# Attention into a mish FFN on one core: another order for the opening, one weight piece in halves, a third probability buffer

## The chip, the cores and the metric

One core of one Trainium2 chip runs the whole program. The metric is the device time of one execution in microseconds (us). Five engines work side by side, each through its own list of instructions in order: TensorE (PE in the profile, with PEld for its weight loads), VectorE (DVE), ScalarE (ACT), GpSimd (POOL) and SyncE (SP), which issues the transfers.

## What is computed

Windowed attention over 8 sequences of 576 tokens with 8 heads of 64, then an FFN of 512 to 2048 to 512 with the activation h * tanh(softplus(h)), called mish in the kernel:

```python
    scores = scale * np.matmul(q, k.transpose(0, 1, 3, 2))
    mask = (rel >= 0) & (rel < window)          # rel = query - key, window = 64
    attn = exp(scores - max);  attn = attn / (sum + 1e-09)
    x = (attn @ v), as [4608 tokens, 512]
    h = x @ w_in                                 # w_in [512, 2048]
    g = h * np.tanh(softplus(h))
    out = g @ w_out                              # w_out [2048, 512]
```

The weights reach the kernel as 64-bit floats, and it decodes them itself.

## The kernel before

The 4608 tokens are cut into 12 chunks of 384 tokens. Per chunk there are four attention units, one for each pair of heads; unit i belongs to chunk i // 4 and pair i % 4. A unit runs in these steps (names of the cost table in brackets): scores on PE (`scores`), masking with the row's extreme on DVE (`ttr`, six of 128 columns), exp with the row sum on ACT (`exp`), a reciprocal of the sums (`small`) and the normalisation of the probabilities on DVE (`norm3` for three blocks of 128, `norm6` for six), the transpose of the probabilities (units 0 to 11 on PE, `tr`, and a copy out of PSUM, `pT`; later units by DVE and 12 small transfers), values on PE (`values`), and the split of x into a high part on ACT (`xh`) and a low part on DVE (`xl`), since every large product is made of three products of rounded parts.

The FFN goes over 16 weight pieces f. Piece f holds 128 columns of w_in and the matching 128 rows of w_out. For each chunk c and piece f: h(c,f) is 12 matmuls into one of two PSUM banks (line L440; `hcc` is one quarter of it, the three matmuls that need one pair's x), mish on ACT, the split of the result (g, `gh` and `gl`), and 9 matmuls that add to the chunk's sum (L514, `acc`). Chunk 0 sums into the banks acc, chunk 1 into the banks at, which the attention of the opening uses as well.

A piece is decoded once, in the opening, and stays: `abs` on ACT (L248) or `absv` on DVE (L251), a clamp (L253), a shift (L254), two merges with the words as they came (L256 and L261), a copy of the high part on ACT (L268) and the low part on DVE (L271). wa0 and wa1 are the two work buffers of the decoding. Exp and abs share one table of ACT and mish has another, so that ACT loads a table between them.

From chunk 2 on PE's order is written out by hand. For chunks 0 and 1 it is made by a planner (`Plan.order`): it steps through all operations with the costs in `COST`, gives each free engine the ready operation of the lowest rank, and the order in which operations would start becomes the order of each engine's list. Ranks come from `RANK_U` (attention units), `RANK_W` (pieces) and `r_ffn` (h and sums). `BEHIND[f]` says how many h of chunk 1 stand in the sequence once h(0,f) is in it; `ACT_ABS` is the number of pieces whose absolute value ACT takes; `SWITCH` is the rank that a table load costs an operation. The probabilities lie in a ring of two buffers (`pr0`, `pr1`), and the output rows in three (`o0` to `o2`).

Of the kernel before, what the change touches and what calls it, by code (L numbers as in the profile page):

```python
# [138 lines left out]
def tile_window_attn_mish_ffn(  # L139
# [24 lines left out]

    class Ring:
        def __init__(self, name, n, shape, dtype=F32, space=None):
            self.name = name
            self.tiles = [(space or const).tile(shape, dtype, name=f"{name}{i}", tag=f"{name}{i}") for i in range(n)]
            self.bufs = [Buf() for _ in range(n)]
# [59 lines left out]
    def weights(f, rank, on_act):  # L229
        buf = wbufs[f]  # L230
        a, abuf = wa_ring.take()
        af = a.bitcast(F32)
# [12 lines left out]
        load = add("SP", "issue", load, writes=[buf], rank=rank - 1.5, size=P * 2 * WP * 8,  # L245
                   after=pace or [units[f].scored])
        if on_act:
            x = add("ACT", "abs", lambda: nc.scalar.activation(af, words[1].bitcast(F32), AF.Abs),  # L248
                    reads=[buf], writes=[abuf], rank=rank, table="exp")
        else:  # L250
            x = add("DVE", "absv", lambda: nc.vector.tensor_scalar(a, words[1], 0x7FFFFFFF, None, ALU.bitwise_and),  # L251
                    reads=[buf], writes=[abuf], rank=rank)
# [510 lines left out]
```

## Time and profile before

| what | us |
|---|---|
| median of three runs | 922.49 |
| lowest and highest run | 921.87, 923.55 |
| the profiled execution | 922.28 |
| its span, first to last instruction | 920.5 |
| PE busy in the span | 900.1 (98%) |
| DVE, ACT, POOL busy | 315.7, 357.2, 262.1 |
| table loads on ACT after the first | 57, 73.1 us |

The profiled execution lies 0.21 us below the median and 1.78 us above its own span. Start times in the rows below count from the first instruction. A row of the timeline has start, duration, engine, line, operation, output and inputs, the number of instructions, and in brackets the idle time of the engine before it and what ended it. Durations of PE's rows overlap, since matmuls are pipelined; the differences of start times are what counts. A row of busy time by stretch has its length, busy time of PE, PEld, DVE, ACT and POOL with the number of instructions, the granted PE clock, the share of the transfer engines and GB/s.

### The profile page before, as it was taken

How to read it: one execution, taken by the hardware profiler on the slowest of the kernel's cores; microseconds unless marked ns; L12 is line 12 of the kernel's file. 1: busy time of each engine (PE TensorE's matmuls, PEld its weight loads, DVE VectorE, ACT ScalarE, POOL GpSimd, SP SyncE). 2: the span in 40 equal slices, each digit the busy share in tenths (PEclk: the TensorE clock that was granted, in tenths of full speed). 3: DMA queues.
4: the chain of work that ended last, by engine and by line, in shares of the span. 5: the costliest groups of instructions: out<-in, count | busy, mean ns of one | idle time of the engine just before them, and what ended most of it. 6: DMA issues, size and time to landing. Idle time of an engine off the chain costs nothing.

```text
span 920.5 us, 17007 instructions
## 1 busy us (share of the span) xinstructions
PE 900.1 (98%) x6411; PEld 808.2 (88%) x6411; DVE 315.7 (34%) x970; ACT 357.2 (39%) x958; POOL 262.1 (28%) x337
## 2 busy tenths in 40 slices
PE   6889999999999999999999999999999999999998
PEld 4678998888898998899899989998998999899897
DVE  6989973432314404304124034042141240400000
ACT  6885336744634414415225134143242241411110
POOL 1000000023333323433353244233333532432432
PEclk9799999999999999999999999999999999999999
DMA  8654412222324203312312222132122220110000
GB/s 272 222 200 168 158 72 73 90 81 71 103 59 127 84 20 95 111 26 88 115 28 83 67 82 78 56 94 77 61 88 67 77 82 24 52 37 1 35 1 35
DMA packets 79906, 77.28 MB, mean 84 GB/s; under 512 B 10064, under 2 KB 73296, under 8 KB 77776
## 3 DMA queue, kind: packets, MB, share of 16 engines
q1 hardware_dynamic: 79680, 75.96, 26.0%
q8 instruction: 51, 0.84, 0.4%
q14 instruction: 31, 0.25, 0.1%
q10 hardware_dynamic: 144, 0.23, 0.1%
HBM read 56.10 MB, written 9.44 MB: 71 GB/s over the span
## 4 chain that ended last, share of the span: by engine, by line
PE 92%; DVE 4%; DMA 2%; ACT 2%; issue 0%; SPq 0%; ACTq 0%; DVEq 0%
PE h L440 43%; PE acc L514 39%; PE at L514 4%; PE at L323 2%; PE at L414 2%; DMA st<-w 2%; PE h L414 1%; ACT pr L348 1%; DVE pr L344 1%; PE acc L323 1%; DVE wa L256 1%; DVE pr L357 0%; DVE wa L261 0%; ACT L723 0%; PE h L323 0%; PE acc L414 0%
## 5 line engine op out<-in xcount | busy, mean ns | idle before, releaser
L440 PE MATMUL h<-xh,w 128*128 128x384 f32 x1536 | 407.4, 338 | 2.0 <-ACT t L469 1.5
L514 PE MATMUL acc<-w,g 128*128 128x512 f32 x1224 | 287.8, 390 | 0.0
L440 PEld LDWEIGHTS h<-xh,w 128*128 128x128 f32 x1536 | 280.7, 189 | 7.1 <-ACT t L469 3.2
L514 PEld LDWEIGHTS acc<-w,g 128*128 128x128 f32 x1224 | 229.2, 188 | 48.0 <-issue 0.5
L469 ACT ACTIVATE t<-h 128x384 f32<-128x384 f32 x192 | 94.3, 492 | 448.4 <-PE h L440 448.1
L440 PE MATMUL h<-xl,w 128*128 128x384 f32 x768 | 258.6, 337 | 0.0
L481 POOL TENSOR_SCALAR gx<-t 128x384 fp32r<-128x384 f32 x40 | 20.5, 514 | 563.6 <-ACT t L469 213.9
L440 PEld LDWEIGHTS h<-xl,w 128*128 128x128 f32 x768 | 145.5, 189 | 2.2
L483 POOL TENSOR_TENSOR g<-t,g 128x384 fp32r<-128x384 f32 x120 | 130.5, 1088 | 9.8
L344 DVE CUSTOM_DVE_ANT_0 pr<-at,mask 128x128 f32<-128x128 f32 x150 | 34.6, 285 | 245.4 <-PE at L323 245.4
L514 PE MATMUL acc<-w,gx 128*128 128x512 f32 x360 | 91.4, 398 | 0.0
L481 POOL TENSOR_SCALAR g<-t 128x384 fp32r<-128x384 f32 x120 | 66.8, 557 | 70.2 <-PE acc L514 41.7
L348 ACT ACTIVATE pr<-pr,mx 128x128 f32<-128x128 f32 x204 | 79.3, 391 | 7.4 <-DVE mx L344 7.2
L514 PEld LDWEIGHTS acc<-w,gx 128*128 128x128 f32 x360 | 65.9, 188 | 15.2 <-issue 2.9
L723 ACT ACT_TABLE_LOAD x57 | 73.1, 1283 | 1.0
L344 DVE CUSTOM_DVE_ANT_0 wa<-at,mask 128x128 f32<-128x128 f32 x57 | 13.3, 286 | 126.1 <-PE at L323 126.1
L519 DVE COPY o<-acc 128x512 f32<-128x512 f32 (+1 forms) x22 | 14.4, 654 | 97.0 <-PE acc L514 94.6
L483 POOL TENSOR_TENSOR gx<-t,gx 128x384 fp32r<-128x384 f32 x40 | 40.5, 1013 | 3.3
L357 DVE TENSOR_TENSOR pr<-pr,sm 128x768 f32<-128x768 f32 (+1 forms) x38 | 40.6, 1068 | 0.9
L348 ACT ACTIVATION_READ_ACCUMULATOR pr<-pr,mx 128x1 f32 x204 | 38.4, 188 | 0.0
L323 PE MATMUL at<-k_t,q_t 64*64 64x128 f32 x828 | 34.8, 284 | 2.5 <-DMA k_t<-kT 1.3
L514 PE MATMUL at<-w,g 128*128 128x512 f32 (+1 forms) x147 | 35.7, 392 | 0.0
(71 smaller groups left out, 579.3 us busy)
## 6 DMA issues: line engine op xcount, KB each, us to landing
v_t<-vN SPq DMA_DIRECT2D x48, 384.0 KB, 4.0
st<-w SPq DMA_DIRECT2D x16, 1024.0 KB, 4.9
k_t<-kT SPq DMA_DIRECT2D x47, 224.0 KB, 4.2
q_t<-qT SPq DMA_DIRECT2D x48, 192.0 KB, 4.3
out<-o SPq DMA_DIRECT2D x35, 256.0 KB, 2.3
pT<-pr SPq DMA_DIRECT2D x288, 24.0 KB, 1.8
pT<-wa SPq DMA_DIRECT2D x144, 24.0 KB, 1.8
k_t<-kT ACTq DMA_DIRECT2D x1, 224.0 KB, 3.4
```

The costliest lines, as they stand in the source:

```text
L323: nc.tensor.matmul(t[par * BLK:(par + 1) * BLK, col:col + P], u.q[0][rows, n * BLK:(n + 1) * BLK], u.k[0][rows, n * BLK:n * BLK + P], star ...
L344: x = add("DVE", "ttr", lambda: nc.vector.tensor_tensor_reduce(out=pr[:, j, :], in0=t_s[:, col:col + P], in1=mk, op0=ALU.add, op1=ALU.min, ...
L348: return add("ACT", "exp", lambda: nc.scalar.activation(pr[:, j, :], pr[:, j, :], AF.Exp, bias=mx[:, j:j + 1], scale=-1.0, accum_out=sm[:, ...
L357: return add("DVE", "norm3" if n == NM else "norm6", lambda: nc.vector.tensor_tensor(pr[:, js, :], pr[:, js, :], sm[:, js].unsqueeze(2).to ...
L414: mm = nc.tensor.matmul(o_ps[rows, n * BLK:(n + 1) * BLK], v_t[:, n, rows], pT[:, 2 * par:2 * par + 2, h * NM + m, :], start=True, stop=True)
L440: nc.tensor.matmul(h_ps[:, :CH], ws[f][:, 0, part, cc * P:(cc + 1) * P], xx[:, cc, :], start=cc == 0 and i == 0, stop=cc == NPAIR - 1 and ...
L469: add("ACT", "mish", lambda: nc.scalar.activation(t, h_ps[:, :CH], AF.Mish), reads=[hb], writes=[tb], rank=post, table="mish")
L481: x = add("POOL", "poolgh", lambda: nc.gpsimd.tensor_scalar(g[:, 0, :], t, 1.0, 0.0, ALU.mult, ALU.add), reads=[tb], writes=[gb], rank=post)
L483: add("POOL", "poolgl", lambda: nc.gpsimd.tensor_tensor(g[:, 1, :], t, g[:, 0, :].bitcast(F32), ALU.subtract), reads=[tb], writes=[gb], af ...
L514: nc.tensor.matmul(bank[:, lo:hi], g[:, a, t * P:(t + 1) * P], ws[f][:, 1, n, lo:hi], start=(alone or f == 0) and i == 0, stop=(alone or f ...
L519: return add(eng, 0.15 + (hi - lo) / 1024, lambda: copy(o[:, lo:hi], bank[0][:, lo:hi]), reads=[bank[1]], writes=[ob], rank=-1)
L723: nc.scalar.preload_act_table_set(TABLES[t.load])
```

## The change

All of it lies in what feeds the planner and in chunks 0 and 1.

- New ranks for units and pieces, `BEHIND` with five h of chunk 1 right after h(0,2), costs of 1.05 instead of 1.2 for PE in the first 70 us, `SWITCH` 150 instead of 80.
- Piece 1 is loaded and decoded in two halves of 512 columns, first the w_in half, then the w_out half (`SPLIT`, `RANK_V`). h waits for the first half of a piece, the sum for the second.
- More h blocks are issued by quarters, each with its own wait for one pair's x (`HCC`).
- The pieces whose absolute value ACT takes are a list: 1, 3, 7, 10, 12 to 15. DVE has the others, pieces 0 and 2 among them.
- Units 2 and 3 are normalised on ACT in six instructions of 128 columns (`NORM_ACT`). Which engine copies a transposed tile is set unit by unit (`COPIES`).
- The three output buffers become one tile, and its first 768 columns serve as a third probability buffer until chunk 0 is done (`spare`).
- Fillers: matmuls of the identity, 64 columns wide, into an unused corner of an h bank, where the planner sees PE idle between 10 and 75 us of its own time; ten in all.

The cut diff:

```diff
-SLOW_UNTIL, SLOW = 70.0, 1.2
+WARM = 10.0, 75.0
+SLOW_UNTIL, SLOW = 70.0, 1.05
...
-SWITCH = 80.0
+SWITCH = 150.0
...
-    o_ring = Ring("o", 3, [P, DO])
-    wa_ring = Ring("wa", 2, [P, 2 * WP], U32)
+    o_ring = Ring("o", 1, [P, 3 * DO])
+    spare = o_ring.tiles[0][:, :HM * P]
+    o_ring.tiles, o_ring.bufs = [o_ring.tiles[0][:, i * DO:(i + 1) * DO] for i in range(3)], [Buf() for _ in range(3)]
+    pr_ring.extend([spare], [Buf()])
+    wa_ring = Ring("wa", 2, [P, 2 * WP], U32, parts=2)
...
+        halves = [[0], [1]] if f in SPLIT else [[0, 1]]
+        for half, rank in zip(halves, ranks):
+            part(f, half, rank, on_act, a, af, abufs, tiles, pace)
...
+            if u.n in NORM_ACT:
+                for j in range(js.start, js.stop):
+                    x = add("ACT", "normb", lambda j=j: nc.scalar.activation(
+                        pr[:, j, :], pr[:, j, :], AF.Copy, scale=sm[:, j:j + 1]), after=[x], rank=rank, reads=[mxb, smb])
+                return x
...
-                x = add("PE", "hcc", lambda cc=cc: emit(cc), reads=[xbufs[c % 2][cc], wbufs[f]], writes=[hb],
+                x = add("PE", "hcc", lambda cc=cc: emit(cc), reads=[xbufs[c % 2][cc], wbufs[f][0]], writes=[hb],
...
-                          reads=[gb, wbufs[f]], writes=[acc[t][1] for t in part], rank=rank, chain=chain,
+                          reads=[gb, wbufs[f][1]], writes=[acc[t][1] for t in part], rank=rank, chain=chain,
...
+    SPLIT = (1,)
+    ACT_ABS = (1, 3, 7, 10, 12, 13, 14, 15)
+    HCC = ((0, 0), (0, 1), (0, 2), (0, 3), (1, 0), (1, 2), (1, 3))
-    RANK_U = [0, 1, 4, 6, 2, 3, 16, 36]
+    RANK_U = [31.4, 31.7, 24.9, 51.0, 12.2, 55.7, 42.6, 55.1, 141.9, 163.3, 136.7, 197.1]
...
+    COPIES = [x.split() for x in ("DVE DVE", "DVE ACT", "ACT ACT", "ACT ACT", "DVE DVE", "ACT ACT", "ACT ACT", "DVE ACT", "ACT DVE", "ACT ACT", "DVE DVE", "ACT DVE")]
+    NORM_ACT = (2, 3)
...
-    ACT_ABS = 7
...
-    BEHIND = [max(0, min(f, 6), f - 8) for f in range(NF)]
+    BEHIND = [0, 1, 5, 5, 5, 5, 7, 7, 7, 8, 8, 8, 8, 8, 8, 8]
...
-        ffn_in(c, f, r_ffn(c, f), False, c == 0 and f < 2)
+        ffn_in(c, f, r_ffn(c, f), False, (c, f) in HCC)
...
+        if t.engine == "PE" and WARM[0] < t.start < WARM[1]:
+            for _ in range(int(0.6 * t.idle / COST["warm"])):
+                nc.tensor.matmul(H[0][0][:, CH:CH + BLK], ident, ident[:, :BLK], start=True, stop=True)
```

The new program has its own line numbers: L369 for the masking, L276 to L297 for the decoding, L387 for the normalisation on DVE, L408 for transposes, L413 for their copies, L444 for values, L458 for xl, L470 for h, L499 for mish, L507 and L508 for g, L544 for the sums, L754 for table loads.

Three places in the lists show the moves. The first is DVE around the normalisation of unit 7, the last of chunk 1 (`pr` is its probability buffer, `st` a piece as it came, `w` the finished piece). Before:

```order
L261 SCALAR_TENSOR_TENSOR wa_115<-st,wa_115 128x1024
L253 TENSOR_SCALAR wa_116<-wa_116 128x1024
L254 TENSOR_SCALAR wa_116<-wa_116 128x1024
L256 SCALAR_TENSOR_TENSOR wa_116<-st,wa_116 128x1024
L354 TENSOR_SCALAR sm_101<-sm_101 128x6
L355 RECIPROCAL sm_101<-sm_101 128x6
L261 SCALAR_TENSOR_TENSOR wa_116<-st,wa_116 128x1024
L357 TENSOR_TENSOR pr_96<-pr_96,sm_101 128x768
```

Now, at the same place in DVE's list:

```order
L281 SCALAR_TENSOR_TENSOR wa_113<-st,wa_113 128x1024
L458 TENSOR_TENSOR xl_118<-at_124,xh_117 128x384
L285 SCALAR_TENSOR_TENSOR wa_113<-st,wa_113 128x1024
L279 TENSOR_SCALAR wa_114<-wa_114 128x512
L379 TENSOR_SCALAR sm_101<-sm_101 128x6
L380 RECIPROCAL sm_101<-sm_101 128x6
L281 SCALAR_TENSOR_TENSOR wa_114<-st,wa_114 128x512
L387 TENSOR_TENSOR pr_95<-pr_95,sm_101 128x768
```

The end of piece 2 and the whole of piece 3 stood ahead of the normalisation (L357); now it is the end of piece 2 and a part of piece 1's second half (L387).

The second place is PE from the transposes of unit 7 to its values. Before (h of piece 2 for chunk 0 stands between, then values, then the sum of piece 1):

```order
L378 MATMUL at_126<-ident,pr_96 128x128 x3
L378 MATMUL at_124<-ident,pr_96 128x128 x3
L440 MATMUL h_127<-xh_117,w 128x384
L440 MATMUL h_127<-xl_118,w 128x384
L440 MATMUL h_127<-xh_117,w 128x384 x2
L440 MATMUL h_127<-xl_118,w 128x384
L440 MATMUL h_127<-xh_117,w 128x384 x2
L440 MATMUL h_127<-xl_118,w 128x384
L440 MATMUL h_127<-xh_117,w 128x384 x2
L440 MATMUL h_127<-xl_118,w 128x384
L440 MATMUL h_127<-xh_117,w 128x384
L414 MATMUL at_125<-pT_104,v_t_94 64x64 x12
```

Now:

```order
L408 MATMUL at_124<-ident,pr_95 128x128 x3
L408 MATMUL at_122<-ident,pr_95 128x128 x3
L470 MATMUL h_125<-xh_115,w 128x384
L470 MATMUL h_125<-xl_116,w 128x384
L470 MATMUL h_125<-xh_115,w 128x384 x2
L470 MATMUL h_125<-xl_116,w 128x384
L470 MATMUL h_125<-xh_115,w 128x384
L470 MATMUL h_126<-xh_117,w 128x384
L470 MATMUL h_126<-xl_118,w 128x384
L470 MATMUL h_126<-xh_117,w 128x384
L444 MATMUL at_123<-pT_104,v_t_94 64x64 x12
```

Instead of a whole h of chunk 0, half of one (h_125) and a quarter of h(1,0) stand there (h_126, with chunk 1's xh_117 and xl_118).

The third place is ACT behind the opening, where mish and the copies of the split follow each other (t is mish's output). Before:

```order
L469 ACTIVATE t_106<-h_127 128x384
L268 CAST w<-wa_115 128x2x512
L477 CAST g_109<-t_106 128x384
L469 ACTIVATE t_107<-h_128 128x384
L477 CAST g_110<-t_107 128x384
L469 ACTIVATE t_108<-h_127 128x384
L268 CAST w<-wa_116 128x2x512
```

Now:

```order
L499 ACTIVATE t_106<-h_125 128x384
L507 CAST g_109<-t_106 128x384
L754 ACT_TABLE_LOAD
L273 ACTIVATE wa_114<-st 128x1024
L294 CAST w<-wa_113 128x2x512
L754 ACT_TABLE_LOAD
L499 ACTIVATE t_107<-h_126 128x384
L507 CAST g_110<-t_107 128x384
```

An absolute value (L273) with a table load on each side now stands between two mish; there are six such places among the later pieces, and 66 table loads in the program where there were 58, the first one counted.

More of the change, by code (lines that the diff above doesn't have):

```diff
@@ L163, in tile_window_attn_mish_ffn, with joined, __init__ @@
     ctx.enter_context(tc.manual_schedule())
+    def joined(bufs):
+        b = Buf()
+        b.writers, b.readers = [t for x in bufs for t in x.writers], [t for x in bufs for t in x.readers]
+        return b
     class Ring:
[L166 to L169, printed above, removed]
+        def __init__(self, name, n, shape, dtype=F32, parts=1):
+            self.tiles = [const.tile(shape, dtype, name=f"{name}{i}", tag=f"{name}{i}") for i in range(n)]
+            self.bufs = [[Buf() for _ in range(parts)] if parts > 1 else Buf() for _ in range(n)]
             self.next = 0
@@ L243, in load, with cost @@
                 tc.add_manual_dep(d.ins, t.ins.name, SYNC, reason="pace")
-        load = add("SP", "issue", load, writes=[buf], rank=rank - 1.5, size=P * 2 * WP * 8,
-                   after=pace or [units[f].scored])
+        def cost(name):
+            return COST[name] if n == 2 else 0.05 + COST[name] / 2
+        add("SP", "issue", load, writes=bufs, rank=rank - 1.5, size=P * n * WP * 8, after=pace or [units[f].scored])
         if on_act:
-            x = add("ACT", "abs", lambda: nc.scalar.activation(af, words[1].bitcast(F32), AF.Abs),
-                    reads=[buf], writes=[abuf], rank=rank, table="exp")
-        else:
-            x = add("DVE", "absv", lambda: nc.vector.tensor_scalar(a, words[1], 0x7FFFFFFF, None, ALU.bitwise_and),
-                    reads=[buf], writes=[abuf], rank=rank)
@@ L253, in weights @@
-        x = add("DVE", "ts", lambda: nc.vector.tensor_scalar(af, af, BIG, TINY, ALU.min, ALU.max), after=[x], rank=rank)
-        x = add("DVE", "ts", lambda: nc.vector.tensor_scalar(a, a, 3, 0x3FFFFFFF, ALU.logical_shift_left, ALU.bitwise_and),
+            x = add("ACT", cost("abs"), lambda: nc.scalar.activation(af, words[1].bitcast(F32), AF.Abs),
+                    reads=bufs, writes=abufs, rank=rank, table="exp")
+        else:
+            x = add("DVE", cost("absv"), lambda: nc.vector.tensor_scalar(a, words[1], 0x7FFFFFFF, None, ALU.bitwise_and),
+                    reads=bufs, writes=abufs, rank=rank)
@@ L257, in weights @@
                 after=[x], rank=rank)
[L258 removed]
         def low():
[L261 to L264 removed]
+            task.ins = nc.vector.scalar_tensor_tensor(a, words[0], 29, a, ALU.logical_shift_right, ALU.bitwise_or).ins
+        x = task = used[f] = add("DVE", cost("stt"), low, after=[x], rank=rank)
         def high():
[L267 to L268 removed]
@@ L270, in weights @@
-        x = add("ACT", "wh", high, after=[x], rank=rank, reads=[abuf])
-        add("DVE", "stt", lambda: nc.vector.tensor_tensor(ws[f][:, :, 1, :], af2, ws[f][:, :, 0, :].bitcast(F32), ALU.subtract),
-            after=[x], rank=rank, reads=[abuf], writes=[buf])
-        return load
+            t = const.tile([P, n, 2, WP], F32R, name="w", tag=tag)
+            for k, i in enumerate(half):
+                tiles[i] = t[:, k]
+            words.append(t)
+            nc.scalar.copy(t[:, :, 0, :], af2)
@@ L275, in load_qk @@
+        x = add("ACT", cost("wh"), high, after=[x], rank=rank, reads=abufs)
+        add("DVE", cost("stt"), lambda: nc.vector.tensor_tensor(words[2][:, :, 1, :], af2, words[2][:, :, 0, :].bitcast(F32), ALU.subtract),
+            after=[x], rank=rank, reads=abufs, writes=bufs)
     def load_qk(u, c, p, rank):
```

73 lines of the change are left out of this document (38 added, 35 removed).

## Prediction

> **What bounds the kernel now.** I read the page's slices first, then busy time by stretch, then the instructions of TensorE (PE), VectorE (DVE) and ScalarE (ACT) one by one over the first 80 us.
>
> ```profile
> PE   6889999999999999999999999999999999999998
> DVE  6989973432314404304124034042141240400000
> PEclk9799999999999999999999999999999999999999
> ```
> Each digit is the busy tenth of a 23 us slice. TensorE is short of full only in the first three slices and at the very end; VectorE is full exactly there (slices one to five); the granted TensorE clock is below full there too.
>
> ```profile
> 0.00:60.00 60.00, 44.61 (x486) 35.41 (x486) 48.56 (x169) 47.21 (x136) 4.24 (x17) 0.86 0.74 243
> 60.00:72.00 12.00, 10.76 (x55) 9.62 (x55) 10.04 (x13) 8.99 (x13) 0.00 (x0) 1.00 0.48 176
> 72.00:900.00 828.00, 827.85 (x5795) 749.17 (x5796) 255.87 (x787) 299.42 (x808) 251.70 (x312) 1.00 0.23 72
> 900.00:920.50 20.50, 16.88 (x78) 14.01 (x76) 1.27 (x3) 1.56 (x3) 6.11 (x8) 0.97 0.11 39
> ```
> From 72 us on, TensorE is busy 827.85 of 828 us: nothing in the order of that part can give more than 0.15 us back. The first 60 us hold 44.61 us of TensorE work at a mean clock of 0.86, and 15.4 us of idle time. A shorter opening therefore moves the whole rest of the program forward one for one, and that is the only place where this change can gain much. The question is when TensorE's unbroken stream begins, and how much of it is already done by then.
>
> ```profile
> 52.04 1.35 PE L378 MATMUL at<-ident,pr 128*128 128x128 f32 x6 [1.85 <-DVE pr L357]
> 53.04 0.67 PE L440 MATMUL h<-xh,w 128*128 128x384 f32 x1
> ...
> 56.52 0.92 PE L414 MATMUL at<-pT,v_t 128*64 128x64 f32 x24
> 57.37 2.34 PE L514 MATMUL acc<-w,g 128*128 128x512 f32 x9
> 60.68 0.44 PE L440 MATMUL h<-xh,w 128*128 128x384 f32 x1 [0.97 <-ACT t L469]
> ...
> 71.95 0.44 PE L440 MATMUL h<-xh,w 128*128 128x384 f32 x1 [0.57 <-ACT t L469]
> ```
> The attention of chunk 1's last head pair ("unit 7") ends the opening: its probabilities are transposed at 52.04, right after a wait of 1.85 us for VectorE's normalisation (L357); twelve h matmuls of the third w piece stand from 53.04 to 56.52 while the transposed tile is copied out; its values run to 57.37. After that TensorE has work queued, and loses only 0.97 us and 0.57 us in two waits for mish, and the slower restarts after them:
>
> ```profile
> 60.68 4.43 PE h L440 x24
> ...
> 80.50 4.18 PE h L440 x24
> ```
> 24 h matmuls take 4.18 us in a full stream and 4.43 after a wait. So before loses, behind unit 7, 0.97 + 0.57 + 2 x 0.25, and 0.28 in the L514 group at 57.37 (2.34 against the 2.04 to 2.08 of the same group later): 2.3 us.
>
> Why does unit 7 come so late? VectorE:
>
> ```profile
> 47.03 0.69 DVE L253 TENSOR_SCALAR wa<-wa 128x1024 f32<-128x1024 f32 x1
> 47.75 0.69 DVE L254 TENSOR_SCALAR wa<-wa 128x1024 uint32<-128x1024 uint32 x1
> 48.48 1.23 DVE L256 SCALAR_TENSOR_TENSOR wa<-st,wa 128x1024 uint32<-128x1024 uint32 x1
> 49.62 0.17 DVE L354 TENSOR_SCALAR sm<-sm 128x6 f32<-128x6 f32 x1
> ...
> 49.93 1.18 DVE L261 SCALAR_TENSOR_TENSOR wa<-st,wa 128x1024 uint32<-128x1024 uint32 x1
> 51.03 0.95 DVE L357 TENSOR_TENSOR pr<-pr,sm 128x768 f32<-128x768 f32 x1
> 51.90 0.55 DVE L428 TENSOR_TENSOR xl<-at,xh 128x384 fp32r<-128x384 f32 x1
> 52.37 2.44 DVE L271 TENSOR_TENSOR w<-wa,w 128x1024 fp32r<-128x1024 f32 x2
> 54.73 0.55 DVE L478 TENSOR_TENSOR g<-t,g 128x384 fp32r<-128x384 f32 x1
> ...
> 74.80 0.68 DVE L251 TENSOR_SCALAR wa<-st 128x1024 uint32<-128x1024 uint32 x1
> 75.52 0.69 DVE L253 TENSOR_SCALAR wa<-wa 128x1024 f32<-128x1024 f32 x1
> ```
> No bracket stands behind these rows: VectorE waits for nothing from 47 to 55 us. The difference of two start times is what an operation costs here: 0.72 us for a clamp or shift (L253, L254, L251), 1.14 and 1.10 for the two merges (L256, L261), 1.18 for the low part (L271 twice in 2.36), 0.87 for a normalisation of 768 columns (L357) and 0.47 for a pass over 384 columns (L428, the nearest row for a normalisation of 384 and for a copy). Unit 7's normalisation, ending at 51.90, queues behind the decoding of the fourth piece (L253 to L261).
>
> **The change, term by term.** *VectorE ahead of unit 7's normalisation.* I counted both orders up to that instruction. The 48 score rows, 12 reciprocals, four wide normalisations, six xl and one g are the same. Different are: four normalisations of 384 (units 2 and 3) go to ACT, -4 x 0.47 = -1.9; the absolute value of pieces 0 and 2 comes from ACT, +2 x 0.72 = +1.4; one copy more, +0.5; eight clamps and shifts become four whole and four half, eight merges four whole and three half, two low parts one whole and one half. A half pass (512 columns) is not in the trace. Its bounds are half the whole and the whole; 0.87 for 768 and 0.47 for 384 columns give 0.40 per 384 and 0.07 fixed, so 0.60 for a half merge or low part, and I take 0.40 for a half clamp (between 0.36 and 0.72). That makes -4 x 0.72 + 4 x 0.40 = -1.3, -4 x 1.12 + 3 x 0.60 = -2.7 and -1.18 + 0.60 = -0.6. Sum: -4.6 us. With halves at the price of wholes only one merge would be saved, -1.1; with halves at exactly half it is -4.8.
>
> ```profile
> 12.78 0.56 DVE L383 COPY pT<-h 128x384 f32<-128x384 f32 x1 [0.98 <-PE h L378]
> 17.31 0.17 DVE L354 TENSOR_SCALAR sm<-sm 128x3 f32<-128x3 f32 x1 [0.83 <-ACT pr L348]
> ```
> VectorE's waits before 52 us are 5.99 us at the start and some 2.9 us in six pieces, of which these two are the longest. A third probability buffer takes pieces like the 0.98 away, since the next unit's score rows need no longer wait for a transpose. New waits arise: unit 7's score rows now stand behind 18 h matmuls and two transposes on TensorE, and its exps on ACT behind a copy that waits for another transpose. Between 0 and 4 us; I take 1.5 more than before. The normalisation then ends at 51.9 - 4.6 + 1.5 = 48.8.
>
> *From there to the end of unit 7's values.* Before, 51.90 to 57.37, where the next group starts, 5.5 us, with twelve h matmuls in between (3.48 us, 53.04 to 56.52, at the half clock). Now nine: 5.5 - 0.9 = 4.6, but the copy of unit 7's first half now stands on ACT behind a table load, a mish and a weight copy; +0.4. End at 53.8, a gain of 3.6.
>
> *What is done by then.* Before 36 h matmuls and nine of L514; now 39 and nine, 3 x 4.18 / 24 = 0.5 us ahead.
>
> *Behind unit 7.* Pieces 0, 1 and 2 are complete and both chunks have x, so five blocks of h and as many sums can run; the third weight's stream is no longer thinned by chunk 0 alone. I take 0.6 us of loss (0 to 2.5) for the 2.3 of before: 1.7.
>
> Sum: 3.6 + 0.5 + 1.7 = 5.8 us of a span of 920.5, hence 914.7. The profiled execution took 922.28, 1.8 above its span and 0.2 below the median of 922.49: forecast 916.5.
>
> *Terms at nothing.* ACT's twelve normalisations of 128 columns (nearest row: an exp of that shape) cost it about 3.6 us, less two absolute values of 1.14 and two copies; they fall into its own waits:
>
> ```profile
> 14.61 1.14 ACT L248 ACTIVATE wa<-st 128x1024 f32<-128x1024 f32 x1 [2.46 <-DMA st<-w]
> 25.98 1.05 ACT L268 CAST w<-wa 128x1024 fp32r<-128x1024 f32 x1 [2.08 <-DVE wa L261]
> 41.19 1.28 ACT L723 ACT_TABLE_LOAD   x1
> 42.49 0.49 ACT L469 ACTIVATE t<-h 128x384 f32<-128x384 f32 x1
> 43.78 1.28 ACT L723 ACT_TABLE_LOAD   x1
> 45.07 1.17 ACT L248 ACTIVATE wa<-st 128x1024 f32<-128x1024 f32 x1
> ```
> 2.46 and 2.08 us of waiting at 14 and 24 us; without that cover they would delay unit 4's exps. The ten fillers of 64 columns sit where TensorE waits and are under 0.15 us each (values of that shape: 0.92 us for 24 passes, two passes each, doubled at half clock). On SP's queue v of unit 0 goes behind q and k of unit 1, and piece 1 comes as two loads of 512 KB: the same bytes, v is wanted only at 13 us. The output rows that share a buffer with unit 6's probabilities are written after chunk 0's last sum, which needs piece 15 (decoded near 133 us, row further below), and those are read by 55.
>
> *A rule that speaks against the change.* The program has 66 table loads where it had 58. In the rows above a load and the instruction behind it start 1.30 and 1.29 us apart. The Trainium skill ("ScalarE: Activation LUTs", "What ACT_TABLE_LOAD costs") gives about 1283 ns for the load and about 1380 ns of drain behind it, 2.66 us per switch. The load agrees with the trace, the drain does not show in it. By the page eight more switches would hold ACT 21 us, by the rows 10 us, in a stretch where ACT is busy about half.
>
> **Rivals.** *Slower: ACT in the weight stage, 75 to 135 us.*
>
> ```profile
> 75.00:135.00 60.00, 60.00 (x303) 54.41 (x303) 56.88 (x70) 24.43 (x40) 0.00 (x0) 1.00 0.39 141
> 132.19 1.23 DVE L271 TENSOR_TENSOR w<-wa,w 128x1024 fp32r<-128x1024 f32 x1 [1.12 <-ACT w L268]
> ```
> ACT is busy 24.43 of these 60 us now. The absolute values of pieces 7, 10 and 12 to 15 come to it, each between two table loads: 1.29 + 1.17 + 1.29, some with a weight copy of 1.05, 3.8 to 4.8 us in which no mish runs. An h bank is wanted again after the other h (2.09) and two sums (4.1), 6.2 us; where only one sum stands between, after 4.15. A sandwich of 4.8 with its mish (0.49) is over that by 1.1, and each stall costs a slow restart of 0.25. It decides when all six fall in short places: 6 x 1.35 = 8.1 us, more than the 5.8 gained, 924.6. Against it: most h come in pairs with two sums behind. Chance 0.05, 924.3 to 926. The page's drain makes this a case of its own: a sandwich would be overdue in the long places too. By that page it is 2.66 + 1.17 + 2.66 + 1.05 + 0.49 = 8.0, over 6.2 by 1.8 six times, about 927. Since 1.30 stands in the rows, 0.01.
>
> *Same: the gain given back by late weights.* VectorE has the same sum of work up to the last piece in both orders (my counts differ by 0.1 us), so piece 15 is complete near 133 us as in the last row above, while TensorE wants it sooner. Ahead of its first use stand 24 h and 23 sums in the new order, less 3 1/4 h and one sum done by 53.8: 20.75 x 2.09 + 22 x 2.06 = 88.7, so 142.5. It decides when the pieces come 9 us later than that. 0.06, at 920.6 to 924.
>
> *Weaker: TensorE's clock.*
>
> ```profile
> 50.00:52.00 2.00, 0.19 (x1) 0.00 (x0) 2.00 (x4) 1.98 (x3) 0.00 (x0) 1.00 0.98 366
> 52.00:54.00 2.00, 1.96 (x9) 1.85 (x10) 2.00 (x3) 1.99 (x5) 0.00 (x0) 0.57 0.84 228
> 54.00:56.00 2.00, 2.00 (x9) 2.00 (x8) 1.28 (x2) 1.98 (x3) 0.00 (x0) 0.57 0.91 377
> 56.00:58.00 2.00, 2.00 (x31) 1.59 (x30) 0.76 (x2) 1.87 (x3) 0.00 (x0) 1.00 0.07 25
> ```
> A pause (TensorE busy 0.19 of 2 us) is followed by 4 us at 0.57. The opening now asks TensorE for more in less time: between the first h matmul at about 34 us and 54 us some 14.6 us of full-speed work. At half clock throughout the middle, unit 7 ends near 56.5, 2.7 later: 919.2. Chance 0.16, 918.6 to 920.6.
> *Stronger.* With short pauses filled the clock stays up, none of the 1.5 and 0.4 us of new waits shows, and unit 7 ends at 51.5: 914 or less. 0.14, 912 to 914.5.
>
> **How the numbers follow.** The forecast itself has 0.58, with its own range 914.5 to 918.6. About 0.2% (1.8 us) is what a measurement of this kernel can tell from no change, so the bound is 920.6. Faster: 0.58 + 0.16 + 0.14 = 0.88; within it 0.06 (given back); slower 0.06 (0.05 + 0.01). The range takes in the forecast, weaker and stronger but for its lowest end: 912.6 to 920.6.
>
> **What would show it.** TensorE busy without a gap from about 55 us, against 72; unit 7's normalisation near 49 and its last xl near 55, against 60.3; f0's low part later than before (33 against 29 us) and no harm from it; 65 table loads outside the start and no TensorE wait for mish over 1 us between 75 and 140. Wrong it would be if score rows of units 6 and 7 wait several us for TensorE at half clock, or if TensorE waits for mish in the weight stage.

## The result and the profile after

The kernel after takes 912.27 us (median of four runs, 911.76 to 912.99) where the one before takes 922.77 (921.87 to 923.55) beside it: a ratio of 0.9887, 95% interval 0.9872 to 0.9903. That is 10.5 us less where 5.8 was forecast, and 0.3 us below the range. The profiled execution took 912.55 with a span of 910.8, 9.7 us under the span of before; the working below goes by these two spans.

The slices of the page, each digit the busy tenth of 23 us:

```profile
PE   6899999999999999999999999999999999999998
DVE  6999974432421412404304124034042240300000
PEclk9999999999999999999999999999999999999999
```
TensorE is now full in the third slice (8 before), and its clock shows no drop in the first three. Busy time by stretch (length, PE, PEld, DVE, ACT, POOL, clock, DMA share, GB/s):

```profile
0.00:60.00 60.00, 48.79 (x551) 40.79 (x552) 51.14 (x178) 47.51 (x149) 4.22 (x17) 0.97 0.77 243
60.00:72.00 12.00, 12.00 (x62) 10.87 (x61) 11.90 (x17) 5.24 (x9) 0.00 (x0) 1.00 0.48 176
72.00:900.00 828.00, 827.85 (x5789) 747.98 (x5788) 249.20 (x776) 315.94 (x819) 256.82 (x320) 1.00 0.23 72
900.00:910.80 10.80, 7.22 (x35) 5.99 (x33) 1.27 (x3) 1.06 (x2) 0.48 (x1) 0.98 0.20 73
```
The first 60 us hold 48.79 us of TensorE work (44.61 before), the next 12 are full (10.76 before), and from 72 to 900 us both kernels have 827.85. By 72 us TensorE has done 105 h matmuls and 54 of the sums, where the kernel before had done 73 and 36; at 4.18 us for 24 h and 2.06 for nine of the sums that is 9.7 us of work. So the whole gain lies in the opening, as the prediction said. TensorE's timeline around unit 7:

```profile
45.36 0.88 PE L408 MATMUL at<-ident,pr 128*128 128x128 f32 x6
...
48.30 0.92 PE L444 MATMUL at<-pT,v_t 128*64 128x64 f32 x24
49.15 0.44 PE L470 MATMUL h<-xh,w 128*128 128x384 f32 x1
...
57.89 0.45 PE L470 MATMUL h<-xh,w 128*128 128x384 f32 x1 [0.62 <-ACT t L499]
```
Unit 7's values end at 49.15 instead of 57.37, 8.2 us sooner, with 39 h matmuls and nine sums done (36 and nine before). Behind it one pause of 0.62 us is left. VectorE's timeline, with half passes (512 columns) among the rows:

```profile
31.18 1.22 DVE L297 TENSOR_TENSOR w<-wa,w 128x1024 fp32r<-128x1024 f32 x1
...
34.51 0.68 DVE L297 TENSOR_TENSOR w<-wa,w 128x512 fp32r<-128x512 f32 x1
...
42.86 0.42 DVE L279 TENSOR_SCALAR wa<-wa 128x512 uint32<-128x512 uint32 x1
43.19 0.17 DVE L379 TENSOR_SCALAR sm<-sm 128x6 f32<-128x6 f32 x1
43.40 0.19 DVE L380 RECIPROCAL sm<-sm 128x6 f32<-128x6 f32 x1
43.50 0.65 DVE L281 SCALAR_TENSOR_TENSOR wa<-st,wa 128x512 uint32<-128x512 uint32 x1
44.07 0.95 DVE L387 TENSOR_TENSOR pr<-pr,sm 128x768 f32<-128x768 f32 x1
...
50.61 0.55 DVE L458 TENSOR_TENSOR xl<-at,xh 128x384 fp32r<-128x384 f32 x1
```
Unit 7's normalisation starts at 44.07 (51.03 before), its last xl at 50.61 (60.28 before). By start times a half shift (L279, the same price as a clamp in the prediction) costs 0.33 us and a half merge 0.57. What VectorE did up to that normalisation, before and then after:

```profile
0.00:51.03 51.03, 36.94 (x435) 28.89 (x435) 41.56 (x160) 38.41 (x126) 4.24 (x17) 0.87 0.76 247
```
```profile
0.00:44.07 44.07, 33.74 (x437) 28.03 (x437) 36.51 (x158) 36.28 (x133) 4.22 (x17) 0.96 0.78 242
```
Busy 41.56 of 51.03 us, then 36.51 of 44.07: 5.1 us less work and 1.9 us less idle time. Before, the idle time is 5.99 us at the start and five pieces, 2.9 us in all: 0.27 at 7.62, the 0.98 and the 0.83 shown in the prediction, and these two:

```profile
8.35 0.29 DVE L344 CUSTOM_DVE_ANT_0 pr<-at,mask 128x128 f32<-128x128 f32 x1 [0.35 <-PE at L323]
...
15.79 0.69 DVE L253 TENSOR_SCALAR wa<-wa 128x1024 f32<-128x1024 f32 x1 [0.46 <-ACT wa L248]
```
Now it is 6.05 us at the start and this one piece:

```profile
12.56 0.29 DVE L369 CUSTOM_DVE_ANT_0 pr<-acc,mask 128x128 f32<-128x128 f32 x1 [1.00 <-PE acc L348]
```
From 17.31 us before, and from 12.56 now, no row of VectorE up to unit 7's normalisation has a wait. The waits that went away lie in the first 18 us, and none came in their place between there and unit 7. ScalarE up to its last exp of unit 7, which the normalisation needs, before and then after (ACT is the fourth pair of numbers):

```profile
0.00:49.50 49.50, 36.24 (x433) 28.69 (x434) 40.06 (x157) 36.90 (x124) 4.24 (x17) 0.86 0.75 242
```
```profile
0.00:43.14 43.14, 32.81 (x433) 27.41 (x434) 35.61 (x155) 35.35 (x132) 4.22 (x17) 0.96 0.78 246
```
and what it waited for in these stretches, before and then after (total, times, longest):

```profile
ACT pr L348 <- DVE mx L344: 7.2, 7, 4.3
ACT wa L248 <- DMA st<-w: 2.5, 1, 2.5
ACT w L268 <- DVE wa L261: 2.1, 1, 2.1
```
```profile
ACT o L373 <- DVE mx L369: 4.9, 2, 4.4
ACT pr L373 <- DVE mx L369: 1.8, 1, 1.8
```
ScalarE's last exp of unit 7 ends 6.36 us sooner. Only 1.55 of that is less work (36.90 to 35.35); 4.8 is less waiting (12.6 to 7.8). The waits for a weight transfer (2.5) and for a merge of VectorE (2.1) are gone. The first of them reached VectorE: piece 0's absolute value waited 2.46 us for its transfer, the exps of the rows behind the 0.83 stood behind it on ScalarE, and VectorE waited 0.46 for the absolute value and 0.83 for the exps. The second (at 25.98) shows in no wait of VectorE. In both kernels the reciprocal step starts within 0.15 us of unit 7's last exp (49.50 to 49.62, 43.14 to 43.19), while VectorE is busy up to that step. So both lists arrive there close together; which of them holds unit 7 these rows don't tell.

### The profile page after: what moved, and what is told of

Read it like the earlier page. It is cut to its first block, busy times and chain, and to the rows that moved or that the text cites. A ratio compares the mean times of both kernels' runs of the same rounds, so it can differ in the third digit from the quotient of the medians.

```text
span 910.8 us, 17071 instructions
## 1 busy us (share of the span) xinstructions
PE 895.9 (98%) x6431; PEld 805.6 (88%) x6431; DVE 313.5 (34%) x972; ACT 369.8 (41%) x979; POOL 261.5 (29%) x337
## 4 chain that ended last, share of the span: by engine, by line
PE 93%; DVE 4%; DMA 2%; ACT 1%; issue 0%; SPq 0%; ACTq 0%; DVEq 0%
PE h L470 43%; PE acc L544 39%; PE at L544 4%; PE at L348 2%; PE at L444 2%; PE h L444 1%; DMA k_t<-kT 1%; DMA st<-w 1%; PE acc L348 1%; DVE pr L369 1%; ACT L754 0%; PE h L348 0%; DVE wa L285 0%; DVE wa L281 0%; PE acc L444 0%; DVE pr L387 0%
## 5 line engine op out<-in xcount | busy, mean ns | idle before, releaser
L470 PE MATMUL h<-xh,w 128*128 128x384 f32 x1536 | 403.9, 336 | 0.9 <-ACT t L499 0.8
L544 PE MATMUL acc<-w,g 128*128 128x512 f32 x1224 | 287.3, 390 | 0.0
L470 PEld LDWEIGHTS h<-xh,w 128*128 128x128 f32 x1536 | 278.6, 188 | 4.6 <-ACT t L499 2.0
L499 ACT ACTIVATE t<-h 128x384 f32<-128x384 f32 x192 | 94.2, 492 | 441.7 <-PE h L470 441.5
L544 PEld LDWEIGHTS acc<-w,g 128*128 128x128 f32 x1224 | 229.3, 188 | 47.7 <-issue 0.5
L470 PE MATMUL h<-xl,w 128*128 128x384 f32 x768 | 257.2, 335 | 0.0
L470 PEld LDWEIGHTS h<-xl,w 128*128 128x128 f32 x768 | 144.2, 188 | 2.6 <-DVE xl L458 0.3
L369 DVE CUSTOM_DVE_ANT_0 pr<-at,mask 128x128 f32<-128x128 f32 x138 | 31.8, 285 | 249.1 <-PE at L348 249.1
L544 PE MATMUL acc<-w,gx 128*128 128x512 f32 x360 | 91.4, 398 | 0.0
L754 ACT ACT_TABLE_LOAD x65 | 83.4, 1283 | 1.1
L544 PEld LDWEIGHTS acc<-w,gx 128*128 128x128 f32 x360 | 65.9, 188 | 15.2 <-issue 2.9
L373 ACT ACTIVATE pr<-pr,mx 128x128 f32<-128x128 f32 x192 | 74.4, 390 | 2.0 <-DVE mx L369 1.8
L369 DVE CUSTOM_DVE_ANT_0 wa<-at,mask 128x128 f32<-128x128 f32 x57 | 13.4, 286 | 122.1 <-PE at L348 122.1
L387 DVE TENSOR_TENSOR pr<-pr,sm 128x768 f32<-128x768 f32 (+1 forms) x32 | 37.2, 1162 | 0.9
L544 PE MATMUL at<-w,g 128*128 128x512 f32 (+1 forms) x147 | 36.5, 395 | 0.0
L373 ACT ACTIVATION_READ_ACCUMULATOR pr<-pr,mx 128x1 f32 x192 | 36.0, 188 | 0.0
```

Source lines behind the costliest of these rows:

```text
L369: x = add("DVE", "ttr", lambda: nc.vector.tensor_tensor_reduce(out=pr[:, j, :], in0=t_s[:, col:col + P], in1=mk, op0=ALU.add, op1=ALU.min, ...
L373: return add("ACT", "exp", lambda: nc.scalar.activation(pr[:, j, :], pr[:, j, :], AF.Exp, bias=mx[:, j:j + 1], scale=-1.0, accum_out=sm[:, ...
L387: return add("DVE", "norm3" if n == NM else "norm6", lambda: nc.vector.tensor_tensor(pr[:, js, :], pr[:, js, :], sm[:, js].unsqueeze(2).to ...
L470: nc.tensor.matmul(h_ps[:, :CH], ws[f][0][:, part, cc * P:(cc + 1) * P], xx[:, cc, :], start=cc == 0 and i == 0, stop=cc == NPAIR - 1 and ...
L499: add("ACT", "mish", lambda: nc.scalar.activation(t, h_ps[:, :CH], AF.Mish), reads=[hb], writes=[tb], rank=post, table="mish")
L544: nc.tensor.matmul(bank[:, lo:hi], g[:, a, t * P:(t + 1) * P], ws[f][1][:, n, lo:hi], start=(alone or f == 0) and i == 0, stop=(alone or f ...
```

## Experiments

"Order kept" means that the planner is replaced by its own finished list, so that nothing moves but what the edit names; "replanned" means that the planner makes a new order. In the runs on fillers and in the doubled one the planner still runs, but sees nothing changed and makes the same order. The expectations name theories by letters and say what each holds. Times are medians; the kernel before took 922.80 to 923.49 beside them, and chips differ, so that steps below 1 us are read only between kernels of one chip.

**Fillers.** The kernel after without them, the kernel before with them, and later the first again beside the kernel after on one chip.

```diff
-        if t.engine == "PE" and WARM[0] < t.start < WARM[1]:
-            for _ in range(int(0.6 * t.idle / COST["warm"])):
-                nc.tensor.matmul(H[0][0][:, CH:CH + BLK], ident, ident[:, :BLK], start=True, stop=True)
```


> The new kernel without its ten fillers; every other instruction keeps its place. Theory C (clock): the fillers keep TensorE at full clock in the opening, so that scores, transposes and values come back sooner and VectorE's waits vanish. Then without them the mean clock of the first 60 us falls from 0.97 towards before's 0.86, unit 7's normalisation comes 2 to 4 us later than 44.1, and the time is 914.5 to 917. Theory O (order): the new order and the third buffer take the waits away, and the clock stays up because the pauses are short anyway. Then 912.3 within 0.8, unit 7's normalisation within 0.7 us of 44.1, and the clock at 0.94 or more.

> The kernel before with fillers by the same rule in its own planned pauses (sixteen), nothing else changed. Theory C: its clock in the first 60 us rises from 0.86 to over 0.93 and the time falls to 918.5 to 921. Theory O: the opening is set by VectorE's list and not by TensorE's clock, so 922.5 within 1, even where the clock rises.

> The kernel after without its ten fillers, on the chip of the next three runs. Theory C (fillers keep the clock up, and that is worth time): half clock somewhere between 24 and 34 us and 913.3 or more, 1 us or more above the kernel after on this chip. Rival (the clock in the pauses isn't on the path): within 0.4 us of the kernel after, whatever the clock shows.

> The kernel after, unchanged, as the level for the other three: 912.3 within 0.7.

Without fillers 912.02 (911.96 to 913.21), ratio 0.9883 (0.9869 to 0.9896). The kernel before with 16 fillers: 923.61, ratio 1.0009 (0.9998 to 1.0021), although its clock in the first 60 us rose from 0.86 to 0.91 (unit 7's normalisation 51.77). On one chip, without fillers 912.17 (912.06 to 913.11), as it is 912.89 (911.49 to 913.40). There the clock did fall. By stretch without fillers, then with them (with them it reads 1.00 in the two stretches that follow, too):

```profile
28.00:30.00 2.00, 2.00 (x28) 1.71 (x32) 1.97 (x6) 2.00 (x6) 0.00 (x0) 0.50 0.70 253
30.00:32.00 2.00, 2.00 (x36) 1.67 (x38) 2.00 (x3) 1.61 (x4) 0.00 (x0) 0.50 0.41 140
32.00:34.00 2.00, 2.00 (x22) 1.79 (x19) 2.00 (x15) 1.02 (x4) 0.00 (x0) 0.50 0.87 236
```
```profile
28.00:30.00 2.00, 1.56 (x32) 1.11 (x30) 1.97 (x7) 2.00 (x9) 0.00 (x0) 1.00 0.79 328
```
Some six us at half clock, and unit 7's normalisation starts at 44.26 against 44.24. TensorE has slack there: at half clock its work fills the pauses. The fillers are no part of the gain, and neither is the clock as far as these runs changed it (in the kernel before it rose to 0.91, not to the 0.97 of the kernel after).

**The third probability buffer**, replanned and with the order kept (both with two buffers; the second also without fillers, and with unit 5's score rows and the second half of unit 4's transposes behind unit 3's transposes, as two buffers need it).

```diff
-    o_ring = Ring("o", 1, [P, 3 * DO])
...
-    pr_ring.extend([spare], [Buf()])
+    o_ring = Ring("o", 3, [P, DO])
...
```


> The new kernel with the probability ring of two buffers and the three output buffers of before; the planner orders anew around it. If the third buffer is what takes VectorE's waits away (part of theory O): unit 7's normalisation 1.5 to 3 us later, 914 to 916. If it is worth nothing: 912.3 within 0.8.

> The new kernel without fillers, its order kept instruction by instruction from a list, with two probability buffers instead of three; rows move only where the second buffer forces them (unit 5's six score rows go behind unit 3's transposes). Theory B (the third buffer itself takes VectorE's waits away): unit 7's normalisation 1.5 to 3 us later than 44.2 and 914 to 916. Theory R (the buffer is needed only for this one place): under 1 us, 912 to 913.

Replanned 917.02 (916.35 to 918.5), ratio 0.9936 (0.9924 to 0.9948), with unit 7's normalisation at 52.23; with the order kept 912.71 (911.84 to 914.26), ratio 0.9882 (0.9866 to 0.9898), the normalisation at 43.48. The buffer itself is worth nothing that shows, and the 0.98 us wait of the kernel before is gone with two buffers as well; the 4.7 us of the first run, more than either theory had, are the other order that the planner made without it.

**Work between VectorE and ScalarE.** Normalisation of units 2 and 3 back on VectorE, replanned and kept; absolute values of pieces 0 and 2 back on ScalarE, without and with the fillers; piece 1 whole, without and with them.

```diff
-    NORM_ACT = (2, 3)
+    NORM_ACT = ()
```
```diff
-    ACT_ABS = (1, 3, 7, 10, 12, 13, 14, 15)
+    ACT_ABS = (0, 1, 2, 3, 7, 10, 12, 13, 14, 15)
```
```diff
-    SPLIT = (1,)
+    SPLIT = ()
```


> The new kernel with units 2 and 3 normalised by VectorE again, four passes of 0.47 us; the planner orders anew around it. If VectorE's list alone sets the opening (the sum of the prediction): 1.9 us later, 914.2 within 0.6. If ACT sets it by now, or the six instructions of ACT cost as much as they save: 912.3 within 0.8.

> The new kernel without fillers, order kept, with the twelve normalisations of 128 columns on ACT replaced by four of 384 on VectorE at the same places. By the prediction's sum of VectorE's list: 4 x 0.47 = 1.9 us later, 913.9 within 0.6. If ACT was the later of the two there, less: 912 to 913. If other waits come with it (the 4.1 us seen when the planner ordered anew): 915.5 or more.

> The kernel after without its fillers, order otherwise kept; the absolute values of two weight pieces (0 and 2) go from VectorE to ScalarE: VectorE has two passes of 0.72 us less ahead of unit 7's normalisation, ScalarE two of 1.15 us more. By the prediction's sum on VectorE alone: normalisation of unit 7 about 1.3 us sooner, 910.7. Theory A (ScalarE holds unit 7 as much as VectorE): no gain or a loss, 912 to 913.5, with VectorE waiting on ScalarE for 1 us or more where it waited for nothing.

> The kernel after, order and fillers kept, the absolute values of pieces 0 and 2 on ScalarE. If ScalarE holds unit 7 too: VectorE waits 2 us or more on ScalarE's absolute values and the time is 0.5 to 1.5 us above the kernel after. If the loss of the run without fillers came from the clock: at the kernel after or up to 1.3 us below it.

> The kernel after without its fillers, order otherwise kept; weight piece 1 is decoded whole, at the place of its first half. VectorE then has the second half's passes ahead of unit 7's normalisation. If each us of VectorE's list ahead of unit 7 counts in full: normalisation about 0.9 us later, 912.5 to 913. If halving is worth nothing: 912.0 within 0.4.

> The kernel after, order and fillers kept, weight piece 1 decoded whole at the place of its first half. If a us of VectorE's list ahead of unit 7 counts in full: normalisation of unit 7 about 0.9 us later than in the kernel after and 0.7 to 1.2 us more time. If the 1.3 us of the run without fillers came from the clock: within 0.4 us of the kernel after.

| run | time | ratio (95%) | unit 7's normalisation | VectorE busy up to it |
|---|---|---|---|---|
| without fillers | 912.02 | 0.9883 (0.9869 to 0.9896) | 44.20 | 36.60 |
| norms on VectorE, replanned | 916.33 | 0.9922 (0.991 to 0.9935) | 44.26 | 37.19 |
| norms on VectorE, kept | 914.19 | 0.9897 (0.9882 to 0.9912) | 46.18 | 38.27 |
| abs on ScalarE | 913.73 | 0.9894 (0.9879 to 0.991) | 44.95 | 35.88 |
| abs on ScalarE, fillers | 914.37 | 0.9904 (0.989 to 0.9919) | 45.55 | 35.85 |
| piece 1 whole | 913.62 | 0.9891 (0.9875 to 0.9907) | 45.33 | 37.70 |
| piece 1 whole, fillers | 913.49 | 0.99 (0.9883 to 0.9916) | 44.82 | 37.51 |
| as it is, same chip as those with fillers | 912.89 | 0.9888 (0.9873 to 0.9903) | 44.24 | 36.50 |

In the two replanned runs the start of unit 7's normalisation and the time don't go together. With the norms on VectorE it starts as in the kernel after, and the kernel takes 4 us more; with two buffers it starts at 52.23, later than the 51.03 of the kernel before, and the kernel is still 6 us faster than that one. What TensorE has done by then counts as much: by 72 us these two had done 96 h matmuls and 48 and 43 of the sums, against 105 and 54. At the prices above that is 2.9 and 4.1 us less, and their spans are 2.7 and 4.4 us longer.

ScalarE's stretch to the last exp of unit 7, as it is and then with the absolute values on ScalarE, same chip:

```profile
0.00:43.30 43.30, 31.89 (x433) 26.32 (x434) 35.59 (x155) 35.20 (x132) 4.22 (x17) 1.00 0.78 245
```
```profile
0.00:44.62 44.62, 32.13 (x434) 26.18 (x435) 34.99 (x153) 37.23 (x134) 4.23 (x17) 1.00 0.75 238
```
VectorE has 0.6 us less to do up to the end of the exps, ScalarE 2.0 more (35.20 to 37.23); the exps end 1.3 later, and the kernel takes 1.5 more. By VectorE's work alone it should have gained. A wait is back that the kernel before had too: VectorE's clamp of piece 0 waits for ScalarE's absolute value, where in the kernel after VectorE takes that value itself (another 0.62 follows at 37.10, for piece 2):

```profile
16.32 0.69 DVE L278 TENSOR_SCALAR wa<-wa 128x1024 f32<-128x1024 f32 x1 [0.80 <-ACT wa L273]
```
The same stretch without fillers, and then with the norms on VectorE too:

```profile
0.00:43.26 43.26, 29.49 (x413) 23.66 (x414) 35.70 (x155) 35.30 (x132) 4.22 (x17) 1.00 0.78 245
```
```profile
0.00:45.27 45.27, 31.10 (x413) 25.30 (x414) 37.40 (x159) 32.83 (x120) 4.25 (x17) 0.92 0.75 235
```
ScalarE has 2.5 us less to do, VectorE 1.7 more, and the exps end 2.0 later. So the split stands near its balance: work that moves from either list to the other makes unit 7's normalisation later, by 0.75 to 2.0 us. The halving is worth 0.6 us on one chip (normalisation 0.58 later for 1.0 more work); the ranges of the two runs touch, so the sign is not beyond doubt by time alone.

**Freeing VectorE in the kernel before.** Order kept; piece 3's four passes on VectorE go behind unit 7's normalisation and xl, and its copy on ScalarE (L268) behind unit 7's. In the second run piece 3's absolute value on ScalarE goes behind unit 7's exps too, and piece 2's low part ahead of piece 3's passes.

The moves in the two lists, in short:

```diff
 DVE, before
-L253, L254, L256, L261 (piece 3)
 L357 (unit 7), L428 (unit 7)
+L253, L254, L256, L261 (piece 3)
```
```diff
 ACT, before
-L248 (piece 3)
 L348 (unit 7)
+L248 (piece 3)
```


> The kernel before, its order kept, with one edit: the first four decoding passes of piece 3 (0.72 + 0.72 + 1.13 + 1.10 us) go behind unit 7's normalisation and the xl that follows it, and the ACT copy of piece 3 behind unit 7's copies. The prediction's mechanism: unit 7's normalisation comes 3.7 us sooner. Of that TensorE can use what it has work for: its stream begins sooner, but piece 3 is late instead, so 920 to 922, a gain of 1 to 3. If the opening is set by the whole of VectorE's work and not by the order: 922.8 within 1.

> The kernel before, order otherwise kept; piece 3's passes on VectorE go behind unit 7's normalisation and last x low part, as in the run that moved them alone, and here piece 3's absolute value on ScalarE also goes behind unit 7's exponentials, and piece 2's low part ahead of piece 3's passes. Theory A (in the kernel before ScalarE and VectorE both held unit 7): normalisation of unit 7 about 48.5 (2.5 us sooner), 920 to 921.5. If VectorE's and ScalarE's lists aren't what held it (late products on TensorE do): normalisation at 50 or later and 922.8 within 1.

The first: 924.93 (923.5 to 926.04), ratio 1.0014 (1.0005 to 1.0023), slower by about 1.4 where 1 to 3 us of gain were forecast. VectorE's timeline in it:

```profile
49.58 0.17 DVE L354 TENSOR_SCALAR sm<-sm 128x6 f32<-128x6 f32 x1 [2.21 <-ACT pr L348]
...
50.01 0.96 DVE L357 TENSOR_TENSOR pr<-pr,sm 128x768 f32<-128x768 f32 x1
```
3.5 us of work are gone ahead of the normalisation (38.09 busy against 41.56), and it starts only 1.0 sooner: the rest became a wait of 2.21 for ScalarE's exps. TensorE then waits 3.2 us for piece 2's low part (L271), now behind piece 3's passes. The second: 929.48 (928.74 to 930.16), ratio 1.0063 (1.0048 to 1.0077), slower by 6.1. The absolute value is out of the way, but the exps still wait, now for a copy of a transposed tile (L383) ahead of them, that needs TensorE, and then for a table load, which stood ahead of the absolute value before and follows the copy now (first exp at 47.31, 46.61 before); behind unit 7 a mish stands on ScalarE behind an absolute value that waits for VectorE, and TensorE waits 5.07 us for that mish:

```profile
45.52 0.48 ACT L383 COPY pT<-at 128x384 f32<-128x384 f32 x1 [1.12 <-PE at L378]
46.02 1.28 ACT L723 ACT_TABLE_LOAD   x1
```
```profile
63.02 1.12 ACT L248 ACTIVATE wa<-st 128x1024 f32<-128x1024 f32 x1 [1.49 <-DVE wa L254]
...
65.82 0.49 ACT L469 ACTIVATE t<-h 128x384 f32<-128x384 f32 x1
```
```profile
66.36 0.69 PE L440 MATMUL h<-xh,w 128*128 128x384 f32 x1 [5.07 <-ACT t L469]
```
The normalisation starts at 50.57, not at 48.5. The forecast for it failed, and with it the thought that two moves would do what the new order does. In the kernel before, VectorE (51.0) and ScalarE's exps (49.5) arrive at unit 7 within 1.5 us of each other, so freeing VectorE alone is worth 1.0. Since the table load moved along with the second edit, that run doesn't show whether TensorE's tile holds the exps as a third chain.

**TensorE's load, and the first transfers.** Without fillers, in the same order: scores, transposes and values of units 4 to 7 issued twice (the second result is the same); and, order kept, the transfer of unit 0's v ahead of those of unit 1's q and k.

```diff
     def emit_scores(u):
+      for _ in range(2 if 4 <= u.n < 8 else 1):
         for m in range(NM):
...
-                for m in range(NM):
+                for m in [m for _ in range(2 if 4 <= u.n < 8 else 1) for m in range(NM)]:
...
-        for n in range(NB):
+        for n in [n for _ in range(2 if 4 <= u.n < 8 else 1) for n in range(NB)]:
```
```diff
-PRIO = [0, 1, 4, ...]
+PRIO = [0, 1, 1.5, ...]
```


> The new kernel without fillers in which scores, transposes and values of units 4 to 7 are computed twice over: 4 x 2.5 = 10 us more of TensorE work between 20 and 49 us, as a half clock would add there. Theory K (TensorE is nearly full from 30 us on, so the full clock is what made the prediction's new waits not come): 4 to 8 us later, 916 to 920, with VectorE waiting for scores. Theory S (slack on TensorE): under 1 us, 912 to 913.

> The kernel after without its fillers, order otherwise kept; only the product v of unit 0 is issued on TensorE ahead of q and k of unit 1, as the order of before had it, so that q and k of unit 1 reach VectorE and ScalarE later by that product. Theory W (the change gained more than forecast because the products come in an order in which VectorE waits almost nowhere): VectorE waits 0.5 to 1 us more ahead of unit 7's normalisation and the kernel takes 912.5 to 913. Rival (the list on VectorE alone sets it and early products are absorbed): normalisation of unit 7 stays at 44.2, 912.0 within 0.4.

Doubled: 914.21 (914.12 to 915.85), ratio 0.9902 (0.9884 to 0.992), between the two theories. TensorE's busy time up to 48 us, without and then with the doubling:

```profile
0.00:48.00 48.00, 33.97 (x455) 27.00 (x456) 40.40 (x164) 40.01 (x139) 4.22 (x17) 1.00 0.78 247
```
```profile
0.00:48.00 48.00, 37.97 (x636) 33.08 (x637) 39.44 (x161) 39.40 (x138) 4.24 (x17) 1.00 0.77 244
```
TensorE does 4.0 us more by 48 us; the normalisation moves by 0.4, the time by 2.2. Ahead of the normalisation its slack took nearly all. Behind it stand unit 7's own transposes and values, doubled too, and they end at 51.62 instead of 49.27 on a TensorE that has no pause left there: that is the 2.2. V first: 913.37 (913.05 to 913.97), ratio 0.989 (0.9874 to 0.9906); the normalisation starts at 45.30, and VectorE idles 8.55 us ahead of it (45.30 less 36.75 busy) where the kernel without fillers idles 7.6.

This run has to be read otherwise than its expectation says. q, k and v are inputs, and the program has no product v on TensorE. Entry 2 of the list, the one that changed, is the transfer of unit 0's v (`load_v`, on SP's queue); entries 3 and 4 are the transfers of unit 1's q and k. The lists of all other engines are as they were. SP, TensorE and VectorE in this run, and then the first two in the kernel after:

```profile
1.18 0.42 SPq L313 DMA_DIRECT2D v_t<-vN  x1
6.88 1.56 PE L348 MATMUL at<-k_t,q_t 64*64 64x128 f32 x24 [1.00 <-DMA k_t<-kT]
8.48 0.29 DVE L369 CUSTOM_DVE_ANT_0 pr<-at,mask 128x128 f32<-128x128 f32 x1 [1.08 <-PE at L348]
```
```profile
2.12 1.02 SPq L313 DMA_DIRECT2D v_t<-vN  x2
5.63 1.55 PE L348 MATMUL at<-k_t,q_t 64*64 64x128 f32 x24
```
With v first, as in the kernel before, unit 1's k lands later, TensorE waits for it, and VectorE waits 1.08 us for unit 1's score rows, where the kernel after waits nothing; unit 7's normalisation comes 1.1 us later. So one place in the order of the first transfers is worth 1.1 us at unit 7. The time is 1.2 to 1.35 us above the two runs without fillers, on other chips and with ranges that touch.

No variant beat the kernel after; without its fillers it is as fast.

## Why the prediction was right and wrong

Right: the opening alone matters, the weight stage hides its changes, VectorE's list gets shorter by about 4.6 us, and the kernel gets faster. That unit 7's end sets TensorE's stream holds for these two kernels, since the h matmuls done by then came out as forecast; in the replanned runs, where fewer or more were done, its normalisation alone doesn't tell the time. The range was missed because one term had the wrong sign. (The sum gives 914.7 for the span, so 916.7 for the median; the 916.5 leaves out the 0.2 between the profiled execution and the median, which changes nothing here.)

| term | predicted | measured |
|---|---|---|
| VectorE's list ahead of unit 7's normalisation | 4.6 less | 5.1 less |
| VectorE's waits there | 1.5 more | 1.9 less |
| from its end to the end of unit 7's values | 4.6 + 0.4, where before took 5.5 | 4.2 (44.94 to 49.15) |
| h matmuls done by then | 0.5 | 0.5 |
| behind unit 7 | 1.7 | 1.0 (9.7 less 8.2 less 0.5) |
| gain of the span | 5.8 | 9.7 |

*The step that failed* is "VectorE's waits, 1.5 more than before". It is off by 3.4 of the 3.9 us that the spans differ from the sum; the list adds 0.45, the way to the values 0.8, and the term behind unit 7 takes 0.7 back (its kept pause is the 0.62 at 57.89, with some slow restarts). It lies outside the step's own bounds, too, which were 0 to 4 us more.

The step failed in both of its parts. The new waits that it named did not come: unit 7's score rows behind 18 h matmuls and its exps behind a copy cost VectorE nothing (no wait from 12.56 us on), and even with TensorE's attention work doubled VectorE waits only 0.62 us for score rows at 38.47 and 0.35 for exps at 43.71. And the working let go of waits like the 0.98 only, where all five pieces went, 2.9 us, against one new piece of 1.00. Two of the causes are shown by runs that bring a wait back: the order of the first transfers (1.08 us back, unit 7 1.1 later) and the absolute value of piece 0, which VectorE now takes itself instead of waiting for ScalarE (0.80 back). The 0.98 is gone with two buffers as well, so the third buffer doesn't explain it; which move took it, and which the 0.27 at 7.62, was not isolated.

*Terms at nothing.* The fillers: confirmed. The third buffer, which the working credited with waits like the 0.98: worth nothing by itself. ScalarE's twelve normalisations "fall into its own waits" of 2.46 and 2.08: wrong in its reason. Those two waits do not exist in the new program, so they hid nothing, and the first was no cover either, since VectorE waited behind it. The normalisations are paid for on ScalarE (2.5 us of its work in the run that took them off), and having them there brings unit 7's normalisation 2.0 us sooner. SP's order, "the same bytes": wrong, since the place of unit 0's v in it is worth 1.1 us at unit 7.

*The half price* of 0.40 for a clamp or shift and 0.60 for a merge or low part: 0.33, and 0.57 to 0.60.

*The rivals.* "Weaker", half clock: half clock for some six us moved unit 7 by 0.02 us. "Stronger" came nearest, in its result but not in its reason, since filling pauses did nothing. "Slower": ScalarE is busy 315.94 of the 828 us instead of 299.42, and TensorE waits for mish only the 0.62 us between 50 and 140. The table loads agree: a load and the exp behind it start 1.30 us apart.

```profile
38.68 1.28 ACT L754 ACT_TABLE_LOAD   x1
39.98 0.40 ACT L373 ACTIVATE pr<-pr,mx 128x128 f32<-128x128 f32 x1
```
The Trainium skill ("ScalarE: Activation LUTs", "What ACT_TABLE_LOAD costs") has a drain of about 1380 ns behind the load of about 1283; the load agrees, and the drain does not show here either. "Same": not seen.

*What would show it.* TensorE's last pause ends at 57.89 (72 before; 55 said), f0's low part stands at 31.18 (28 before; 33 said) with no harm, 65 table loads outside the start, as said. The normalisation near 49 and the last xl near 55 came 4 to 5 us sooner than said.

*Open.* Which of the ranks takes away VectorE's 0.98 and ScalarE's wait of 2.1 was not isolated, and no run built the order up from the kernel before: the runs that bring single waits back don't add up to the whole gain.

## What to carry to other kernels

When a queue ahead of the deciding instruction is shortened, look at what its other operand waits for: if another engine's chain ends shortly before, the shortening is worth only that gap (1.0 us for 3.5 us of work here). Reckon the waits of the deciding list one by one, each with what ends it and whether the new order still has it, and don't put an allowance for a busier stretch in their place. The order of the first transfers counts even where the bytes are the same. A variant that goes through a planner measures the planner's new order; pin the order to price one part, and count what the deciding engine has done by a fixed time, not only when one instruction starts.

## What the runs showed of the hardware that was not expected

The same program on the same pause does not always lose its clock. The kernel without fillers had these two rows on two chips (TensorE, start, length, what it waited for):

```profile
26.82 0.85 PE L408 MATMUL at<-ident,pr 128*128 128x128 f32 x6 [2.73 <-ACT o L384]
```
```profile
26.15 0.84 PE L408 MATMUL at<-ident,pr 128*128 128x128 f32 x6 [2.74 <-ACT o L384]
```
After the first the clock read 1.00 in every stretch of 2 us, after the second 0.50 for the six us from 28 to 34. The times were 912.00 and 913.11 for these executions, and 912.02 and 912.17 in the medians. In the kernel before, after a shorter pause of 1.85 us, it read 0.57. The length of one pause does not tell whether the clock falls.
